# One-token decode layer on one core: K and V in 4 MiB tiles of four heads, 32 KiB a partition, with score tiles by token quarter

## The chip, the core and the metric

The kernel runs on one core of one Trainium2 chip. The metric is the device time of one execution in microseconds. The work is done by TensorE (PE, matrix products, with its weight loads shown apart as PEld), VectorE (DVE), ScalarE (ACT) and GpSimd (POOL); SyncE (SP) only issues transfers. Transfers from device memory (HBM) into the on-chip memory (SBUF, 128 partitions) are carried by 16 DMA engines; matrix products land in PSUM, eight banks of 512 fp32 columns a partition.

## The reference

One token for each of B = 4 sequences goes through a layernorm, attention over a cached window, a second layernorm and a gated feed-forward part:

```python
x = A_x                                              # [4, 1, 576]
q = (layernorm(x) @ wq).reshape(B, 1, 32, 128)       # 32 query heads of 128
k = k_cache[:, :, 16384 - 4096:, :]                  # 16 K/V heads, last 4096 tokens,
v = v_cache[:, :, 16384 - 4096:, :]                  #   two query heads share a K/V head
p = softmax(q @ k.T * 128 ** -0.5)
h = x + (p @ v).reshape(B, 1, 4096) @ wo
g = layernorm(h)
out = h + (relu(g @ W_gate) * (g @ W_up)) @ W_down   # 576 -> 4608 -> 576
```

Everything is bfloat16 in memory. K and V of the window are 64 pairs (sequence, head) of 1 MiB each, so 134.2 MB of the 159.6 MB that the kernel reads; the rest are the weights.

## The kernel before

All engines run programs written out by hand. A small scheduler (`Sched`) counts the instructions of each engine and lets an instruction wait for a named earlier one (`deps`). Every large transfer is issued by SP in one fixed order, the list `transfers`, and SP waits at each transfer until the earlier user of its SBUF place is done (`add`, which finds the places that overlap); what stands behind a waiting transfer waits too.

A "duo" is two K/V heads of one sequence: 2 MiB of K or of V, as 128 partitions of 16 KiB. Partition 2p+s holds 64 consecutive tokens (64p to 64p+63) of head s, one contiguous run of HBM; the two heads of a duo lie 4 MiB apart there. There are 32 duos, four places for K duos and four for V duos. The order is wq (4.7 MB), K0 to K4, then V and K in turn with V five duos behind (`VLEAD`), then wo, the gate and up weights, and the down weights in nine pieces. wo takes the places of the first K duos, the gate and up weights those behind them, and the down weights wait for the product with wo (`ATTN`).

For each half of a K duo (`tr`, line 414) DVE transposes 128 x 2048 fp32 words (each word a pair of bf16) in blocks of 32 x 32 into one of `NKT` = 3 buffers `kT`. PE then does eight products of 128 x 512 (`qk`): the weights are `qz`, q put into the columns of its own duo with zeros elsewhere. Four duos (a batch of 8 K/V heads) accumulate into one score tile `sc` of four banks, 128 rows by 2048 columns. After the batch DVE takes the row maximum (`rmax`, line 417), POOL the maximum over partitions (line 293), DVE the bias (`fbias`), ACT four exponentials of 512 with row sums (line 342), DVE transposes the whole tile of 128 x 2048 fp32 (`trp`, line 433) and ACT casts and packs it to bf16 (line 349). The two heads of a duo lie in alternate columns. The scores of the next batch overwrite `sc` and so wait for the exponentials. The product with V (`pv`) runs five duos behind (`PVLAG`): 16 products of 16 x 512 a duo. PE's order is the scores of duo i, then the product with V of duo i-5. For each batch ACT copies the result (`cpy`), PE adds up the four token parts (`ext`), DVE divides by the sum of the exponentials (`norm`, one for each sequence).

Behind the attention: product with wo, second layernorm, gate and up products, down product in the order in which the nine pieces land, output.

All matrix products are issued by one helper, so they share line 518; they are told apart by tile (`sc<-kT,qz` for the scores, `pb<-pool,prob` for the product with V).

Of the kernel before, what the change touches and what calls it, by code (L numbers as in the profile page):

```python
# [7 lines left out]
ALU = mybir.AluOpType  # L8
# [4 lines left out]
B = 4  # L13
# [6 lines left out]
T = WIN // 64  # L20
# [3 lines left out]
NDUO = B * KVH // 2  # L24
NB = 4
NBATCH = NDUO // NB
NHB = 4 * NB
# [3 lines left out]
DUO = 2 * WIN * DH // 128  # L31
NKS = 4
NVS = 4
# [4 lines left out]
VLEAD = 5  # L38
PVLAG = 5
JJ = 9  # L40
BIG = 1.5e38
NG = FC // JJ
# [60 lines left out]
def bass_sequential_preLN__sliding_block_cached__glu_gated_reglu__decode_kernel(  # L103
# [12 lines left out]
    with ExitStack() as es:  # L116
# [4 lines left out]

        pool = sb("pool", [128, (NKS + NVS) * DUO], BF16)
        kT = sb("kT", [128, NKT, DUO // 4], FP32)
# [6 lines left out]
        x_f = sb("x_f", [B, D], FP32)  # L130
        junk_f = sb("junk_f", [B, D], FP32)
# [12 lines left out]
        qz = sb("qz", [128, 2, NB, 4, 128], BF16)  # L144
        mask = sb("mask", [128, 3, NHB], FP32)
        selT = sb("selT", [128, 4, NHB], FP32)
        rmx = sb("rmx", [128, 2, 2], FP32)
        rsel = sb("rsel", [128, 2], FP32)
        bmin = sb("bmin", [128, 2], FP32)
        pmax = sb("pmax", [128, 2, NHB], FP32)  # L150
        bcm = sb("bcm", [128, 2, NHB], FP32)
        t8 = sb("t8", [128, NHB], FP32)
        bias = sb("bias", [128, 2, 2], FP32)
        rs2 = sb("rs2", [128, 2, 4], FP32)
        rs1 = sb("rs1", [128, 2], FP32)
        P = sb("P", [128, T * 32], FP32)
        probT = sb("probT", [128, T, 32], FP32)
        prob = sb("prob", [128, 2, NB, T, 4], BF16)
# [12 lines left out]
        hhT = probT[:, 0:FC // 2, :].bitcast(BF16).rearrange("p f b -> p (f b)")[:, 0:FC * 32].rearrange("p (f b) -> p f b", b=32)  # L171
        S8 = probT[:, FC // 2:FC // 2 + 16, :].bitcast(BF16).rearrange("p f b -> p (f b)")
# [39 lines left out]
        def duo(cache, d):  # L212
# [3 lines left out]
        def add_K(d):  # L216
            s = d % NKS
            add(("K", d), f"kslot{s}", s * DUO, DUO, ("TR", 2 * d + 1),
                lambda e, o: e.dma_start(out=o, in_=duo(A_k_cache, d)))

        def add_V(d):
            s = d % NVS
            add(("V", d), f"vslot{s}", (NKS + s) * DUO, DUO, ("PV", d),
                lambda e, o: e.dma_start(out=o, in_=duo(A_v_cache, d)))
# [3 lines left out]
        add(("wq", 0), "wq0", NKS * DUO, 4 * HQ, "QMM",  # L228
            lambda e, o: e.dma_start(out=o, in_=A_wq[0:512, :].rearrange("(p u) n -> p (u n)", u=4)))
        add(("wq", 4), "wq4", NKS * DUO + 4 * HQ, HQ // 2, "QMM",  # L230
            lambda e, o: e.dma_start(out=o, in_=A_wq[512:576, :].rearrange("r (u n) -> (r u) n", u=2)))
        for m in range(NDUO + VLEAD):
            if m < NDUO:
                add_K(m)
            if m >= VLEAD:
                add_V(m - VLEAD)
# [36 lines left out]
        def prog_pool(S):  # L273
# [15 lines left out]
            for n in range(NBATCH):  # L289
                deps = [("EMAX", n)]  # L290
                if n >= 2:
                    deps.append(("BIAS", n - 2))
                S.op(g, lambda e, n=n: e.partition_all_reduce(bcm[:, n % 2, :], pmax[:, n % 2, :], 128, bass_isa.ReduceOp.max),  # L293
                     deps=deps, name=("PAR", n))


        def prog_act(S):
# [12 lines left out]
            def qzero(n):  # L310
                b, q = divmod(n, 2)
                for g in range(4):
                    deps = []
                    if g == 0:
                        deps = ["D_QR", "QZ0"] if n < 2 else [("QK", 2 * NB * (n - 1) - 1)]
                    src = bass.AP(tensor=qrep, offset=32 * g * 4 * H * B + NHB * q * B + b,
                                  ap=[[4 * H * B, 32], [4 * B, NB], [H * B, 4], [B, 4]])
                    dst = bass.AP(tensor=qz, offset=32 * g * 2 * NB * 512 + (n % 2) * NB * 512 + 32 * g,
                                  ap=[[2 * NB * 512, 32], [512 + 4, NB], [128, 4], [1, 4]])
                    S.op(a, lambda e, src=src, dst=dst: e.copy(out=dst, in_=src), deps=deps,  # L320
                         name=("QZ", n) if g == 3 else None, signal=g == 3)

            def cpy(n):
                deps = [("PV", NB * n + NB - 1)]
                if n >= 2:
                    deps.append(("EXT", n - 2))
                S.op(a, lambda e: e.copy(out=cp[:, n % 2, :], in_=pb[PVB + n % 2]), deps=deps, name=("CP", n))  # L327
# [3 lines left out]
            for n in range(NBATCH):  # L331

                for th in range(2):
                    for u in range(2):
                        deps = []
                        if th == 0 and u == 0:
                            deps = [("BIAS", n)]
                            if n >= 1:
                                deps.append(("TRP", n - 1))
                            if n >= 2:  # L340
                                deps.append(("RSUM", n - 2))
                        S.op(a, lambda e, n=n, th=th, u=u: e.activation(  # L342
                            out=P[:, th * 1024 + u:(th + 1) * 1024:2], in_=sc[:, th * 1024 + u:(th + 1) * 1024:2], func=ACT.Exp,
                            scale=SCALE, bias=bias[:, n % 2, u:u + 1], accum_out=rs2[:, n % 2, 2 * th + u:2 * th + u + 1]),
                            deps=deps, name=("EXP", n, th) if u else None, signal=u == 1)
                deps = [("TRP", n)]
                if n >= 2:
                    deps.append(("PV", NB * (n - 2) + NB - 1))
                S.op(a, lambda e, n=n: e.copy(out=prob[:, n % 2, :, :, :],  # L349
                                              in_=probT[:, :, 0:NHB].rearrange("p t (r x) -> p r t x", x=4)), deps=deps, name=("CMP", n))  # L350
                if n >= 1:
                    cpy(n - 1)
                if n + 2 < NBATCH:
                    qzero(n + 2)
            cpy(NBATCH - 1)
# [8 lines left out]
        def prog_dve(S):  # L364
# [17 lines left out]
            for x in range(2):  # L382
                S.op(v, lambda e, x=x: e.memset(pb[PVB + x], 0.0), name=f"PVZ{x}")

            S.op(v, lambda e: e.tensor_reduce(out=mask[:, 0, :], in_=bass.AP(tensor=ident_b, offset=0, ap=[[128, 128], [1, NHB], [32, 4]]),
# [6 lines left out]
            for u in range(2):  # L392
                S.op(v, lambda e, u=u: e.tensor_reduce(out=rsel[:, u:u + 1], in_=mask[:, 1, :].rearrange("p (r s h) -> p s r h", s=2, h=2)[:, u, :, :],
                                                       axis=AX.XY, op=ALU.max), deps=["M1"] if u == 0 else [], name=f"RSEL{u}")
# [12 lines left out]
            def tr(i):  # L407
                deps = [land(("K", i // 2))]
                if i >= NKT:
                    deps.append(("QK", i - NKT))  # L410
                x0 = at[("K", i // 2)] + (i % 2) * (DUO // 2)
                src = pool[:, x0:x0 + DUO // 2].bitcast(FP32).rearrange("p (t c k) -> p c t k", c=2, k=32)
                dst = kT[:, i % NKT, :].rearrange("p (c t k) -> p c t k", c=2, k=32)
                S.op(v, lambda e: e.transpose(out=dst, in_=src), deps=deps, name=("TR", i))  # L414

            def rmax(n):
                S.op(v, lambda e: e.tensor_reduce(out=rmx[:, n % 2, :], in_=sc[:, :].rearrange("p (x u) -> p u x", u=2), axis=AX.X, op=ALU.max),  # L417
                     deps=[("QK", 2 * NB * (n + 1) - 1)], name=("RMAX", n))
                rb = bass.AP(tensor=rmx, offset=(n % 2) * 2, ap=[[4, 128], [0, NB], [1, 2], [0, 2]])
                S.op(v, lambda e: e.tensor_tensor(out=pmax[:, n % 2, :].rearrange("p (r s h) -> p r s h", s=2, h=2),  # L420
                                                  in0=mask[:, 1, :].rearrange("p (r s h) -> p r s h", s=2, h=2), in1=rb, op=ALU.min),
                     deps=[("RMAX", n), "M2"] + ([("PAR", n - 2)] if n >= 2 else []), name=("EMAX", n))

            def fbias(n):
                S.op(v, lambda e: e.scalar_tensor_tensor(out=t8[:, :], in0=bcm[:, n % 2, :], scalar=-SCALE, in1=mask[:, 2, :],
                                                         op0=ALU.mult, op1=ALU.max), deps=[("PAR", n)], name=("T8", n))
                S.op(v, lambda e: e.tensor_reduce(out=bmin[:, n % 2:n % 2 + 1], in_=t8[:, :], axis=AX.X, op=ALU.min),
                     deps=[("T8", n)], name=("BMIN", n))
# [276 lines left out]
```

## Time and profile before

| | us |
|---|---|
| three runs of the kernel before | 382.54, 382.57, 382.62; median 382.57 |
| the profiled execution | 382.39 |
| its span, first to last instruction | 381.1 |
| outside of the span | 1.3 |

The page gives for each engine the time in which it was busy; the span in 40 slices (9.5 us each), with the share in which the 16 DMA engines were busy; the queues of the transfers; the chain of work that ended last, followed back from the end; and groups of instructions with their mean time and with what ended the idle time ahead of them. A query of the trace for the transfers in a stretch gives the packets that started there, their bytes, and the time that they took as a share of 16 engines; a query by stretches gives each engine's busy time and the TensorE clock granted (1.00 is full). Every instruction that moves data has its time in the trace; the ends of matrix products are modelled.

### The profile page before, as it was taken

The page shows a single profiled execution, that of the slowest core. Times are in us where ns is not written, and L with a number is a line of the kernel's source. Part 1 is how long each engine was busy: PE and PEld are TensorE (multiplying, and loading weights), DVE is VectorE, ACT ScalarE, POOL GpSimd, SP SyncE. Part 2 cuts the span into 40 slices and gives each one's busy share as a digit, 9 for nine tenths or more (in the row PEclk, how much of TensorE's full clock was granted, in tenths as well). Part 3 has the DMA queues.
Part 4 walks back from the last instruction along what each step waited for, and adds up shares of the span by engine and source line. Part 5 has one row for each costly group of instructions (what it writes and reads, how often), then busy time and mean ns, then how long its engine had stood idle before and what let it go on. Part 6 is the DMA issues. An engine that isn't in the chain of part 4 may idle for free.

```text
span 381.1 us, 3911 instructions
## 1 busy us (share of the span) xinstructions
PE 284.2 (75%) x1701; PEld 124.4 (33%) x1716; DVE 206.3 (54%) x193; ACT 53.5 (14%) x129; POOL 8.2 (2%) x22
## 2 busy tenths in 40 slices
PE   0059749976996699669957995799779996945474
PEld 0053213322432243224322432243224333435341
DVE  0259789369447754774487548644775443042021
ACT  4012050021102110211031103100310021010020
POOL 4100000000000000000000000000000000000000
PEclk9999969998999899989998999899859997975669
DMA  8999999999999999999999999999999999999995
GB/s 331 409 430 428 426 435 420 434 423 428 431 423 433 423 430 425 428 430 426 430 426 428 430 426 425 432 425 430 426 428 432 421 433 420 420 444 432 414 411 227
DMA packets 11985, 159.84 MB, mean 419 GB/s; under 512 B 1336, under 2 KB 1472, under 8 KB 2624
## 3 DMA queue, kind: packets, MB, share of 16 engines
q1 hardware_dynamic: 11960, 159.59, 98.8%
q8 instruction: 13, 0.21, 0.2%
q14 instruction: 4, 0.03, 0.0%
q10 hardware_dynamic: 8, 0.00, 0.0%
HBM read 159.58 MB, written 0.00 MB: 419 GB/s over the span
## 4 chain that ended last, share of the span: by engine, by line
DMA 34%; PE 33%; DVE 20%; issue 5%; ACT 5%; SPq 1%; POOL 1%; POOLq 0%
DMA pool<-in_A_k_cache_dram 27%; PE pb L518 17%; PE sc L518 16%; DVE kT L414 11%; DMA pool<-in_B_W_down_dram 7%; ACT P L342 4%; DVE probT L433 3%; DVE rmx L417 3%; SPq L254 1%; POOL bcm L293 1%; DVE P L475 1%; DVE P L471 0%; DVE bias L429 0%; DVE sel L374 0%; ACT cp L327 0%
## 5 line engine op out<-in xcount | busy, mean ns | idle before, releaser
L414 DVE STREAM_TRANSPOSE kT<-pool 128x2048 f32<-128x2048 f32 x64 | 144.2, 2290 | 55.8 <-DMA pool<-in_A_k_cache_dram 52.9
L518 PE MATMUL sc<-kT,qz 128*128 128x512 bf16 x497 | 132.1, 418 | 50.2 <-DVE kT L414 46.7
L518 PE MATMUL pb<-pool,prob 128*16 128x512 bf16 x512 | 116.5, 388 | 0.0
L518 PEld LDWEIGHTS sc<-kT,qz 128*128 128x128 bf16 x512 | 48.6, 101 | 130.7 <-DVE kT L414 57.6
L518 PEld LDWEIGHTS pb<-pool,prob 128*16 128x16 bf16 x512 | 43.7, 91 | 70.1 <-issue 16.4
L342 ACT ACTIVATE P<-sc,bias 128x512 f32<-128x512 f32 x32 | 22.2, 720 | 174.9 <-DVE bias L429 174.9
L417 DVE TENSOR_REDUCE rmx<-sc 128x2 f32<-128x2048 f32 x8 | 18.3, 2291 | 32.2 <-PE sc L518 32.2
L433 DVE STREAM_TRANSPOSE probT<-P 128x2048 f32<-128x2048 f32 x8 | 18.5, 2312 | 7.9 <-ACT P L342 7.9
L525 PE MATMUL pb<-ident_b,xn_bf 4*128 4x4 bf16 (+1 forms) x5 | 0.4, 180 | 20.8 <-ACT xn_bf L306 20.8
L327 ACT COPY cp<-pb 128x512 f32<-128x512 f32 x8 | 4.7, 585 | 68.3 <-PE pb L518 68.3
L518 PE MATMUL pb<-selT,cp 128*128 128x16 f32 x64 | 8.6, 267 | 4.3 <-ACT cp L327 4.3
L442 DVE RECIPROCAL rs_sb<-pb 128x32 f32<-128x32 f32 x4 | 1.4, 338 | 18.0 <-PE pb L518 18.0
L349 ACT CAST prob<-probT 128x1024 bf16<-128x1024 f32 x8 | 8.4, 1045 | 19.0 <-DVE rs L436 19.0
L518 PEld LDWEIGHTS pb<-selT,cp 128*128 128x128 f32 x64 | 8.9, 205 | 6.3 <-ACT cp L327 5.3
L505 DVE TENSOR_TENSOR P<-pb,P 128x288 bf16<-128x288 f32 (+1 forms) x2 | 0.8, 402 | 17.5 <-PE pb L518 17.5
L518 PE MATMUL sc<-oX,pool 128*128 128x4 bf16 (+1 forms) x160 | 6.6, 177 | 3.7 <-DVE oX L478 3.7
L293 POOL PARTITION_ALL_REDUCE bcm<-pmax x8 | 3.1, 388 | 290.0 <-DVE pmax L420 290.0
L518 PE MATMUL pb<-pool,hnT 128*32 128x288 bf16 (+1 forms) x48 | 4.4, 408 | 6.4 <-DMA pool<-in_B_W_up_dram 6.4
L320 ACT COPY qz<-qrep 32x64 bf16<-32x64 bf16 x32 | 7.8, 244 | 7.3 <-DVE qrep L451 7.0
L518 PE MATMUL pb<-pool,probT 128*4 128x288 bf16 x72 | 5.7, 285 | 4.0 <-DMA pool<-in_B_W_down_dram 3.4
L518 PE MATMUL sc<-pool,hnT 128*32 128x288 bf16 (+2 forms) x112 | 7.3, 375 | 1.4 <-DMA pool<-in_B_W_gate_dram 1.4
L518 PEld LDWEIGHTS sc<-oX,pool 128*128 128x128 bf16 (+1 forms) x160 | 6.5, 123 | 3.9 <-issue 3.8
(107 smaller groups left out, 79.9 us busy)
## 6 DMA issues: line engine op xcount, KB each, us to landing
pool<-in_A_k_cache_dram SPq DMA_DIRECT2D x32, 2048.0 KB, 28.7
pool<-in_A_v_cache_dram SPq DMA_DIRECT2D x32, 2048.0 KB, 26.3
pool<-in_A_wo_dram SPq DMA_DIRECT2D x4, 1152.0 KB, 21.4
pool<-in_B_W_gate_dram SPq DMA_DIRECT2D x1, 4608.0 KB, 23.9
pool<-in_B_W_up_dram SPq DMA_DIRECT2D x1, 4608.0 KB, 29.4
pool<-in_A_wq_dram SPq DMA_DIRECT2D x1, 4096.0 KB, 13.2
pool<-in_B_W_down_dram SPq DMA_DIRECT2D x2, 1296.0 KB, 22.9
pool<-in_B_W_down_dram SPq DMA_DIRECT2D x5, 432.0 KB, 25.5
```

What stands on the lines that cost most here:

```text
L254: lambda e, g0=g0, g1=g1, j0=j0, nj=nj: e.dma_start(out=wd_sb[:, g0:g1, j0 * D:(j0 + nj) * D], in_=B_W_down[g0 * 128 * JJ:g1 * 128 * JJ, : ...
L293: S.op(g, lambda e, n=n: e.partition_all_reduce(bcm[:, n % 2, :], pmax[:, n % 2, :], 128, bass_isa.ReduceOp.max), deps=deps, name=("PAR", n))
L320: S.op(a, lambda e, src=src, dst=dst: e.copy(out=dst, in_=src), deps=deps, name=("QZ", n) if g == 3 else None, signal=g == 3)
L327: S.op(a, lambda e: e.copy(out=cp[:, n % 2, :], in_=pb[PVB + n % 2]), deps=deps, name=("CP", n))
L342: S.op(a, lambda e, n=n, th=th, u=u: e.activation(out=P[:, th * 1024 + u:(th + 1) * 1024:2], in_=sc[:, th * 1024 + u:(th + 1) * 1024:2], f ...
L349: S.op(a, lambda e, n=n: e.copy(out=prob[:, n % 2, :, :, :], in_=probT[:, :, 0:NHB].rearrange("p t (r x) -> p r t x", x=4)), deps=deps, na ...
L414: S.op(v, lambda e: e.transpose(out=dst, in_=src), deps=deps, name=("TR", i))
L417: S.op(v, lambda e: e.tensor_reduce(out=rmx[:, n % 2, :], in_=sc[:, :].rearrange("p (x u) -> p u x", u=2), axis=AX.X, op=ALU.max), deps=[( ...
L433: S.op(v, lambda e: e.transpose(out=probT[:, :, :].rearrange("p t j -> p (t j)"), in_=P[:, :]), deps=[("EXP", n, 1)] + ([("CMP", n - 1)] i ...
L442: S.op(v, lambda e: e.reciprocal(out=rs_sb[:, b, :], in_=pb[OB][:, 64 + b * H:64 + (b + 1) * H]), deps=[("SUM", b)], name=("RS", b))
L475: S.op(v, lambda e: e.tensor_reduce(out=oS.rearrange("p (x b) -> p x b", b=B), in_=oM.rearrange("p (x s b) -> p x b s", s=8, b=B), axis=AX ...
L518: S.op(t, lambda e: e.matmul(o, lhsT=l, rhs=r, start=start, stop=stop, skip_group_check=skip), deps=deps, name=name, signal=name is not None)
```

## The change

- **Tiles.** A "quad" is four K/V heads of one sequence: 4 MiB, 128 partitions of 32 KiB. Partition 4p+s holds 128 consecutive tokens of head s. There are 16 quads and four places of 4 MiB, shared by K and V in the order of the list; the place of a K quad is given back by its fourth transpose, that of a V quad by its product. V is one quad behind K. At the end of the list V13 lies in place 0, K15 in 1, V14 in 2 and V15 in 3; wo goes over places 0 and 1, the gate weights over 1 and 2, the up weights over 2 and 3.
- **Scores.** Each of the four quarters of a K quad is transposed as before (128 x 2048 words, into three buffers) and gives eight products of 128 x 512, all into the same two banks: quarter j of the tokens is written to the rows 32a + 8j + (query head). A quad so has one score tile of 128 x 1024, and two tiles take turns in the four banks. Columns of the four heads lie interleaved.
- **Mask.** Ahead of each tile's products two products of `foe` (4 x 128) and `col` (4 x 512) write a large negative number where the row's head is not the column's head, so the exponential gives zero there. Before, foreign columns were left out by separate exponentials and biases.
- **Softmax by tile.** Maximum over 1024 columns, maximum over partitions, bias, one exponential of 1024 to bf16 with the row sum, one transpose of 128 x 1024 in bf16 into one of four buffers. The cast and packing on ACT, the second bias and the sum of four row sums are gone.
- **Product with V.** 32 products a quad, weights of 128 x 32, the moving operand four runs of 128 columns (one from each quarter of the partition); the result of a sequence (4 quads) fills one bank. Copy, `ext` and `SUM` come once for each sequence.
- `x_f` and `junk_f` now lie in `P`, which is free at that time. The places and the order of wo, gate, up and down weights keep their offsets in SBUF.

```diff
-        pool = sb("pool", [128, (NKS + NVS) * DUO], BF16)
+        pool = sb("pool", [128, NSLOT * QUAD], BF16)
...
-            b, m = divmod(d, KVH // 2)
-            return cache[b, 2 * m:2 * m + 2, SK - WIN:SK, :].rearrange("s (p t) d -> p s (t d)", p=64)
+            b, m = divmod(i, NPB)
+            return cache[b, NS * m:NS * m + NS, SK - WIN:SK, :].rearrange("s (p t) d -> p s (t d)", p=32)
...
+        slots = iter(range(2 * NQUAD))
+
+        def add_K(i):
+            x = next(slots) % NSLOT
+            add(("K", i), f"slot{x}", x * QUAD, QUAD, ("TR", 4 * i + 3),
+                lambda e, o: e.dma_start(out=o, in_=quad(A_k_cache, i)))
+
+        def add_V(i):
+            x = next(slots) % NSLOT
+            add(("V", i), f"slot{x}", x * QUAD, QUAD, ("PV", i),
...
+        for m in range(NQUAD + VLEAD):
+            if m < NQUAD:
                 add_K(m)
             if m >= VLEAD:
                 add_V(m - VLEAD)
...
+            for i in range(NQUAD):
+                deps = [("BIAS", i)]
+                if i >= 2:
+                    deps += [("TRP", i - 2), ("RSUM", i - 2)]
+                S.op(a, lambda e, i=i: e.activation(
+                    out=Pb[:, (i % 2) * 1024:(i % 2 + 1) * 1024], in_=sc[:, (i % 2) * 1024:(i % 2 + 1) * 1024], func=ACT.Exp,
+                    scale=SCALE, bias=bias[:, i % 2:i % 2 + 1], accum_out=rs1[:, i % 2:i % 2 + 1]),
+                    deps=deps, name=("EXP", i))
+                if i + 2 < NQUAD:
+                    qzero(i + 2)
+                if i >= NPB and i % NPB == 0:
+                    cpy(i // NPB - 1)
...
+            def trp(i):
+                b, m = divmod(i, NPB)
+                S.op(v, lambda e: e.transpose(out=pT[i % NPT], in_=Pb[:, (i % 2) * 1024:(i % 2 + 1) * 1024]),
+                     deps=[("EXP", i)] + ([("PV", i - NPT)] if i >= NPT else []), name=("TRP", i))
...
+            for i in range(NQUAD):
+                for j in range(4):
+                    tr(i, j)
...
+                rmax(i)
+                fbias(i)
+                trp(i)
+                if i > NPB and i % NPB == VLEAD:
+                    norm(i // NPB - 1)
...
+            def qk(i, j):
+                f = 4 * i + j
+                bank = 2 * (i % 2)
+                deps = [("TR", f)]
+                if j == 0:
+                    for half in range(2):
+                        mm(pb[bank + half], foe[:, :], col[:, :], True, False, deps=(["COL"] if i == 0 else [("EXP", i - 2)] if i >= 2 else []) if half == 0 else [])
+                    deps.append(("QZ", i))
+                for ce in range(4):
+                    c, e = divmod(ce, 2)
+                    for half in range(2):
...
+            def pv(i):
+                b, r = divmod(i, NPB)
+                x0 = at[("V", i)]
+                vv = pool[:, x0:x0 + QUAD].rearrange("p (q t d) -> p t q d", q=4, d=DH)
+                deps = [("TRP", i), land(("V", i))]
+                if r == 0 and b >= 2:
+                    deps.append(("CP", b - 2))
+                for t_ in range(TQ // 4):
...
+            for i in range(NQUAD + VLEAD):
+                if i < NQUAD:
+                    for j in range(4):
+                        qk(i, j)
+                if i >= VLEAD:
+                    j = i - VLEAD
+                    if j % NPB == 0 and j >= NPB:
+                        ext(j // NPB - 1)
+                    pv(j)
```

More of the change, by code (lines that the diff above doesn't have):

```diff
@@ L329, in prog_act, with cpy @@
+            def cpy(b):
+                deps = [("PV", NPB * b + NPB - 1)]
+                if b >= 2:
+                    deps.append(("EXT", b - 2))
+                S.op(a, lambda e: e.copy(out=cp[:, b % 2, :], in_=pb[PVB + b % 2]), deps=deps, name=("CP", b))
             qzero(0)
             qzero(1)
[L331 to L354, printed above, removed]
@@ L416, in rmax @@
[L416 to L422, printed above, removed]
```

262 lines of the change are left out of this document (102 added, 160 removed).

## The prediction

> **What bounds the kernel now.** I read the page's transfers first, then what SP and the engines do around the last V duo.
>
> ```profile
> PE 284.2 (75%) x1701; PEld 124.4 (33%) x1716; DVE 206.3 (54%) x193; ACT 53.5 (14%) x129; POOL 8.2 (2%) x22
> ...
> DMA  8999999999999999999999999999999999999995
> ...
> q1 hardware_dynamic: 11960, 159.59, 98.8%
> ...
> pool<-in_A_k_cache_dram SPq DMA_DIRECT2D x32, 2048.0 KB, 28.7
> pool<-in_A_v_cache_dram SPq DMA_DIRECT2D x32, 2048.0 KB, 26.3
> ```
>
> SP's queue (q1) keeps all 16 DMA engines busy for 98.8% of the span; the missing 1.2% (4.6 us) lie in the first and the last slice. A K or V duo lands 26 to 29 us after its issue, though its own share of the traffic is about 5 us: over 20 us of other transfers always stand ahead of it. PE is busy 75%, DVE 54%. So the time is that of the bytes through the DMA engines, plus start and end, and the waits between engines cost nothing while the queue has a stock. A change can win only by making the transfers cheaper, and lose by letting the queue run dry or making the transfers dearer.
>
> The tail, from the order of instructions in time:
>
> ```profile
> 328.62 0.33 SPq L243 DMA_DIRECT2D pool<-in_B_W_gate_dram  x1
> 334.03 0.59 ACT L327 COPY cp<-pb 128x512 f32<-128x512 f32 x1 [16.06 <-PE pb L518]
> 334.09 0.33 SPq L243 DMA_DIRECT2D pool<-in_B_W_up_dram  x1
> ...
> 340.97 6.63 PE L518 MATMUL sc<-oX,pool 128*128 128x4 bf16 x160 [3.67 <-DVE oX L478]
> 347.63 17.50 SPq L254 DMA_DIRECT2D pool<-in_B_W_down_dram  x9
> ...
> 352.56 0.91 PE L518 MATMUL sc<-pool,hnT 128*32 128x216 bf16 x16 [1.42 <-DMA pool<-in_B_W_gate_dram]
> ...
> 363.52 0.37 PE L518 MATMUL pb<-pool,hnT 128*32 128x216 bf16 x4 [6.42 <-DMA pool<-in_B_W_up_dram]
> ```
>
> The up weights are issued when the last product with V ends (334.1) and land at 363.5; the down weights are issued at 347.6, 16 us ahead of that landing. The end of attention is thus covered by queued weights, and gate, up and down products wait for data.
>
> **The price of a row.** The same query of the transfers for three stretches: one with 16 KiB rows of K and V, one in which 32 KiB rows of wq start, one with mostly 36 KiB rows of gate and up.
>
> ```profile
> DMA packets 7345, 106.97 MB, mean 428 GB/s; under 512 B 815, under 2 KB 815, under 8 KB 815
> ...
> q1 hardware_dynamic: 7336, 106.84, 100.5%
> ```
> ```profile
> DMA packets 65, 2.13 MB, mean 426 GB/s; under 512 B 0, under 2 KB 0, under 8 KB 0
> ...
> q1 hardware_dynamic: 65, 2.13, 98.7%
> ```
> ```profile
> DMA packets 239, 7.78 MB, mean 432 GB/s; under 512 B 19, under 2 KB 19, under 8 KB 27
> ...
> q1 hardware_dynamic: 236, 7.74, 100.3%
> ```
>
> The first is 60 to 310 us: 7336 packets, 815 of them the small end marks of a transfer (16 each), so 6521 rows. They took 1.005 x 16 x 250 = 4020 us of engine time: 616.5 ns a row with its share of the marks. The second is 4 to 9 us: 65 rows took 0.987 x 16 x 5 = 79.0 us, 1215 ns each. The third is 342 to 360 us: 209 rows of 36 KiB (236 less 19 marks and 8 rows of 4.5 KiB) took 1.003 x 16 x 18 = 288.9 us, less some 1.6 us for the small ones, 1374 ns each. A row therefore carries a small fixed cost: 32 KiB cost 2 x 616.5 = 1233 ns in two rows and 1215 in one. If the 36 KiB row is scaled by bytes alone, with no fixed part, 32 KiB cost 1222 ns; that stretch has the engines at work as the K and V stretch has, while at 4 to 9 us PE and DVE stand still.
>
> **The change part by part.**
>
> *Transfers.* 64 issues of 128 rows become 32. Each DMA engine carries 64 x 128 / 16 = 512 rows of K and V now, 256 of double size after. The gain a 32 KiB row is 1233 - 1222 = 11 ns at least and 1233 - 1215 = 18 ns at most; I take 14, between them, since the quiet row is too cheap for a busy stretch and the scaled one leaves out that the fixed part is paid once. The marks are halved too, which is inside the 1233. 256 x 14 ns = 3.6 us (2.8 to 4.6). Half the issues on SP (0.54 to 0.61 us each) are hidden by the stock and gain nothing.
>
> *Does the queue stay full?* A quad's K and V take 16 rows an engine, 16 x 1.219 = 19.5 us. The softmax chain of the second batch, from the chain of work, and the groups:
>
> ```profile
> 74.00 3.74 PE sc L518 x16
> ...
> 77.77 2.30 DVE rmx L417
> ...
> 80.37 0.40 POOL bcm L293
> ...
> 81.46 2.86 ACT P L342 x8
> ...
> 84.35 2.31 DVE probT L433
> ...
> 86.97 2.23 DVE kT L414
> 89.19 0.05 issue
> 89.24 3.37 PE sc L518 x8
> ```
> ```profile
> L414 DVE STREAM_TRANSPOSE kT<-pool 128x2048 f32<-128x2048 f32 x64 | 144.2, 2290 | 55.8 <-DMA pool<-in_A_k_cache_dram 52.9 <-PE sc L518 2.9
> ...
> L508 DVE STREAM_TRANSPOSE probT<-P 128x288 bf16<-128x288 bf16 x4 | 1.9, 478 | 0.1
> ...
> L471 DVE TENSOR_TENSOR P<-sc,mask 128x1024 f32<-128x1024 f32 x1 | 1.2, 1225 | 0.7 <-PE sc L518 0.7
> ```
>
> From the maximum to the next K transpose before takes 86.97 - 77.77 = 9.2 us. After, a tile has half the columns: maximum 1.2 (DVE reads 1024 fp32 of PSUM in 1.225 us), exponential 1.4 (half of 2.86; at most the 2.86), transpose of 1024 bf16 1.25 (the 288 one's 0.48 plus 736 columns at the slope to the 2.31 of 2048; between 1.15 and 2.31), the rest as now less one small step, 1.5: 5.4 us, at most 7.9. DVE's loop over a quad is four transposes of 2.29 (9.2), the products of the fourth quarter (eight, half of 3.74, 1.9) and these 5.4: 16.5 us, 19.0 by the upper ends, under 19.5 both times. PE has 32 score products, 32 with V and 2 masks of about 3.74 / 16 = 0.23 us: 15.4 us. The masks (0.5 us a quad) stand ahead of PE's wait for the first transpose and need only the exponential of two quads earlier, so they lie in PE's idle time; uncovered they would be 16 x 0.47 = 7.5 us. They cannot gain. The moving operand of `pv` in runs of 128 columns and its 32-column weights have no row; the scores read every second element now and go at the same 0.23, so I take no cost. It becomes visible only if 64 such products a quad push PE past 19.5 us, that is at 0.30 us each. The cast, `BMIN`, second bias and `RS1` removed lie beside the stream: nothing.
>
> *The places.* The start, in time order, and the first stretch:
>
> ```profile
> 22.38 2.30 DVE L414 STREAM_TRANSPOSE kT<-pool 128x2048 f32<-128x2048 f32 x1
> ...
> 27.03 0.69 DVE L451 CAST qrep<-sc 128x512 bf16<-128x512 f32 x1 [0.70 <-PE sc L518]
> ...
> 27.76 2.05 ACT L320 COPY qz<-qrep 32x64 bf16<-32x64 bf16 x8 [7.03 <-DVE qrep L451]
> ```
> ```profile
> 0.00:14.00 14.00, 0.00 (x0) 0.00 (x0) 0.58 (x4) 4.30 (x7) 3.88 (x7) 1.00 0.88 349
> ```
>
> Four places of 4 MiB hold the same bytes as eight of 2 MiB. The tightest is the first reuse by K3 (place of K1). wq and five quads stand ahead of it, 25.7 MB: 4.9 in the first 14 us (349 GB/s), the rest at 428 until about 62 us. K0 (wq and 4.2 MB) lands near 24 us rather than 22; q is ready at 27.7 and put into `qz` by some 30, so the fourth quarter's scores end near 38, the chain adds 5.4 and K1's four transposes 9: 53 us, 9 us ahead. With loops of 16.5 against 19.5 this grows. V1 and V2 have 12 us or more.
>
> *The tail.* In the last places wo waits for V13 and K15, gate for V14, up for V15. The last product is one of a quad now, 32 x 0.23 = 7.4 us behind V15's landing, about 4 us later against its data than the duo's 16; up has wo and gate (9.4 MB, 22 us) ahead of it in the queue. The down weights wait for `ATTN`, 13.6 us behind the last product before (334.0 to 347.6), and had 16 us of cover. Cost nothing; without that cover up to 4 us.
>
> Sum: 382.39 - 3.6 = 378.8 for the profiled execution, which lies 0.2 under the median of the runs; so 379.0 for the median, 378.0 to 379.8 by the ends of the row's price.
>
> **The rivals.**
>
> *The stream gets no cheaper.* The 18 ns are then what compute adds to a row in proportion to its bytes (PE and DVE use SBUF beside it), not a price per row; the marks alone are left. The 36 KiB row, measured beside work, speaks against it. Time 382.3: within 0.2%.
>
> *A cold TensorE makes the quad longer than its transfers* (slower). The stretches show the clock falling to half after 3.5 us of idle PE:
>
> ```profile
> 85.75:89.50 3.75, 0.26 (x2) 0.14 (x3) 3.71 (x5) 1.04 (x1) 0.00 (x0) 1.00 1.05 441
> 89.50:92.91 3.41, 3.41 (x9) 0.93 (x8) 3.41 (x2) 0.00 (x0) 0.00 (x0) 0.50 0.96 408
> ```
>
> After the change PE ends its product with V and waits for the next K quad and its first transpose in every quad, some 4 us (19.5 less 15.4), so this can come each 19.5 us rather than each 39. One stretch of 3.41 us at half clock costs 1.7 us of PE work: 17.1 us for PE, 18.2 for the loop, still covered. It decides from two such stretches on in every quad with the upper ends of the chain: 19.0 + 3.4 = 22.4 us, 2.9 over, 16 times 46 us, less the 9 us ahead at the start: 379 + 37 = 416; with the middle of the chain, 16.5 + 3.4 = 19.9, the stock covers it. Half way, 21.2 us a quad, 16 x 1.7 - 9 = 18 us: 397, the time I give it. The stock of two quads and the short idle speak against.
> The Trainium skill, "TensorE: Matmul & The Clock Gate", Part 1, says that an idle window of about 3.4 us throttles the clock to half until a busy one has passed; the trace agrees with 3.75 us ahead of 3.41 at 0.50.
>
> *Four heads make the reads slower* (slower). Rows of neighbouring partitions lie 4 MiB apart in HBM, in pairs now, in fours after, and an engine may have several in flight. That pairs cost nothing visible (616.5 against half of 1215) speaks against, and wq has no such step. A slow 32 KiB row is seen at the start: from 1.5 to 13.5 us the stream made 384 GB/s, against 428 later.
>
> ```profile
> DMA packets 252, 4.61 MB, mean 384 GB/s; under 512 B 19, under 2 KB 23, under 8 KB 124
> ```
>
> If K and V went at that, 134.2 MB would take 349 us, not 314: 382.6 + 35 = 418. It loses as soon as a row costs over 1233 ns.
> The Trainium skill, "DMA: Bandwidth & Descriptors", Latency and other measured facts, gives 103 GB/s for copies with rows 4 MiB apart where 214 is full; by that, an estimate, K and V would take twice as long. The pairs at 428 GB/s here disagree, and no run yet shows four.
>
> **How the numbers follow.** A measurement of this kernel can tell 0.2%, 0.8 us, from no change. The forecast, 379.0, has 0.78; the stream unchanged 0.08; the cold TensorE 0.08; slow reads 0.06. So faster 0.78, same 0.08, slower 0.14. The forecast's own range is 378.0 to 379.8; for 8 in 10 I go down to 377.5 (the shares are read to 0.1%, near 1 ns a row, and the engines end unevenly) and up to 382.6, which takes in the unchanged stream and leaves out the slower cases.
>
> **What would show it.** Right: 32 KiB rows of K and V at 1215 to 1222 ns; q1 again near 98.8% of a shorter span; DVE waiting for K in every quad; up weights issued over 20 us ahead of their landing. Wrong: a slice of DMA under 9 between the first and the last (a dry queue; the time from issue to landing then falls to some 10 us); rows over 1233 ns; half clock in a large part of the slices together with DVE no longer waiting for K.

## The result, and the profile after

| | before | after |
|---|---|---|
| median of the runs, us | 382.56 (382.26 to 382.62, 4 runs) | 380.29 (380.21 to 380.30, 4 runs) |
| ratio, with its 95% interval | | 0.9942 (0.9925 to 0.9959) |
| profiled execution, us | 382.39 | 380.29 |
| its span, us | 381.1 | 379.0 |
| mean TensorE clock | 0.909 | 0.909 |

The kernel became faster by 2.27 us. 3.6 us were forecast.

The page of the kernel after: busy times, the line of the DMA engines over the span, the queue, the chain by engine, the groups that the prediction priced, and the issues of K and of the up weights.

```profile
PE 296.7 (78%) x1716; PEld 129.4 (34%) x1716; DVE 210.2 (55%) x223; ACT 49.5 (13%) x117; POOL 11.0 (3%) x30
...
DMA  8999999999999999999999999999999999999995
...
q1 hardware_dynamic: 7352, 159.59, 98.5%
...
DMA 59%; DVE 22%; PE 14%; ACT 1%; SPq 1%; issue 1%; POOL 0%
...
L404 DVE STREAM_TRANSPOSE kT<-pool 128x2048 f32<-128x2048 f32 x64 | 142.5, 2281 | 38.9 <-DMA pool<-in_A_k_cache_dram 38.6
...
L337 ACT ACTIVATE P<-sc,bias 128x1024 bf16<-128x1024 f32 x16 | 17.8, 1114 | 248.5 <-DVE bias L415 248.5
L407 DVE TENSOR_REDUCE rmx<-sc 128x1 f32<-128x1024 f32 x16 | 19.6, 1225 | 41.2 <-PE sc L497 41.2
L420 DVE STREAM_TRANSPOSE probT<-P 128x1024 bf16<-128x1024 bf16 x16 | 19.9, 1245 | 20.3 <-ACT P L337 20.3
...
L497 PE MATMUL sc<-col,foe 4*128 4x512 bf16 x32 | 10.0, 394 | 0.0
...
pool<-in_A_k_cache_dram SPq DMA_DIRECT2D x16, 4096.0 KB, 29.9
...
pool<-in_B_W_up_dram SPq DMA_DIRECT2D x1, 4608.0 KB, 25.8
```

The queue is still the bound: q1 is busy for 98.5% of a span that is 2.1 us shorter, no slice between the first and the last falls under 9, and the chain that ended last is mostly DMA. The packets of q1 fell from 11960 to 7352 for the same 159.59 MB. DVE waits 38.6 us for K, so compute is not late. PE grew by 12.5 us of busy time (10.0 us are the 32 mask products; the page before has a record of only 497 of the 512 score products), and none of this shows in the time.

The transfers from 60 to 310 us of the kernel after, in the same query that gave 428 GB/s before:

```profile
DMA packets 3708, 107.69 MB, mean 431 GB/s; under 512 B 416, under 2 KB 416, under 8 KB 416
...
q1 hardware_dynamic: 3698, 107.55, 100.1%
```

3698 packets less 416 marks are 3282 rows of 32 KiB. 250 us on 16 engines are 4000 us, so a row, with its share of the marks, occupies an engine for 1218.8 ns.

### The profile page after: what moved, and what is told of

Read it like the earlier page. It is cut to its first block, busy times and chain, and to the rows that moved or that the text cites. A ratio compares the mean times of both kernels' runs of the same rounds, so it can differ in the third digit from the quotient of the medians.

```text
span 379.0 us, 3903 instructions
## 1 busy us (share of the span) xinstructions
PE 296.7 (78%) x1716; PEld 129.4 (34%) x1716; DVE 210.2 (55%) x223; ACT 49.5 (13%) x117; POOL 11.0 (3%) x30
## 3 DMA queue, kind: packets, MB, share of 16 engines
q1 hardware_dynamic: 7352, 159.59, 98.5%
## 4 chain that ended last, share of the span: by engine, by line
DMA 59%; DVE 22%; PE 14%; ACT 1%; SPq 1%; issue 1%; POOL 0%
DMA pool<-in_A_k_cache_dram 53%; DVE kT L404 18%; PE sc L497 10%; DMA pool<-in_B_W_down_dram 6%; PE pb L497 4%; DVE probT L420 1%; DVE rmx L407 1%; ACT P L337 1%; SPq L256 1%; DVE P L454 1%; DVE P L450 0%; ACT qz L322 0%; POOL bcm L295 0%; DVE pmax L409 0%; DVE qrep L436 0%
## 5 line engine op out<-in xcount | busy, mean ns | idle before, releaser
L497 PE MATMUL sc<-kT,qz 128*128 128x512 bf16 x512 | 141.8, 437 | 41.1 <-DVE kT L404 40.0
L404 DVE STREAM_TRANSPOSE kT<-pool 128x2048 f32<-128x2048 f32 x64 | 142.5, 2281 | 38.9 <-DMA pool<-in_A_k_cache_dram 38.6
L497 PE MATMUL pb<-pool,probT 128*32 128x512 bf16 (+1 forms) x584 | 118.9, 368 | 5.3 <-DMA pool<-in_B_W_down_dram 3.9
L497 PEld LDWEIGHTS sc<-kT,qz 128*128 128x128 bf16 x512 | 51.8, 106 | 131.0 <-DVE kT L404 55.6
L497 PEld LDWEIGHTS pb<-pool,probT 128*32 128x32 bf16 (+1 forms) x584 | 50.9, 95 | 71.5 <-DMA pool<-in_B_W_down_dram 7.6
L337 ACT ACTIVATE P<-sc,bias 128x1024 bf16<-128x1024 f32 x16 | 17.8, 1114 | 248.5 <-DVE bias L415 248.5
L407 DVE TENSOR_REDUCE rmx<-sc 128x1 f32<-128x1024 f32 x16 | 19.6, 1225 | 41.2 <-PE sc L497 41.2
L420 DVE STREAM_TRANSPOSE probT<-P 128x1024 bf16<-128x1024 bf16 x16 | 19.9, 1245 | 20.3 <-ACT P L337 20.3
L322 ACT COPY qz<-qrep 32x128 bf16<-32x128 bf16 x64 | 18.8, 294 | 10.4 <-DVE qrep L436 9.8
L504 PE MATMUL pb<-ident_b,xn_bf 4*128 4x4 bf16 (+1 forms) x5 | 0.4, 180 | 19.5 <-ACT xn_bf L308 19.5
L497 PE MATMUL sc<-col,foe 4*128 4x512 bf16 x32 | 10.0, 394 | 0.0
L504 PEld LDWEIGHTS pb<-ident_b,xn_bf 4*128 4x128 bf16 (+1 forms) x5 | 0.3, 115 | 19.5 <-ACT xn_bf L308 19.5
L497 PEld LDWEIGHTS pb<-selT,cp 128*128 128x128 f32 x32 | 4.1, 191 | 1.7 <-ACT cp L329 1.2
## 6 DMA issues: line engine op xcount, KB each, us to landing
pool<-in_A_k_cache_dram SPq DMA_DIRECT2D x16, 4096.0 KB, 29.9
pool<-in_B_W_up_dram SPq DMA_DIRECT2D x1, 4608.0 KB, 25.8
pool<-in_B_W_down_dram SPq DMA_DIRECT2D x2, 1296.0 KB, 19.4
```

Of the source, the lines that this page charges most:

```text
L337: S.op(a, lambda e, i=i: e.activation(out=Pb[:, (i % 2) * 1024:(i % 2 + 1) * 1024], in_=sc[:, (i % 2) * 1024:(i % 2 + 1) * 1024], func=ACT ...
L407: S.op(v, lambda e: e.tensor_reduce(out=rmx[:, i % 2:i % 2 + 1], in_=sc[:, (i % 2) * 1024:(i % 2 + 1) * 1024], axis=AX.X, op=ALU.max), dep ...
L420: S.op(v, lambda e: e.transpose(out=pT[i % NPT], in_=Pb[:, (i % 2) * 1024:(i % 2 + 1) * 1024]), deps=[("EXP", i)] + ([("PV", i - NPT)] if ...
L497: S.op(t, lambda e: e.matmul(o, lhsT=l, rhs=r, start=start, stop=stop, skip_group_check=skip), deps=deps, name=name, signal=name is not None)
```

## The experiments

The theory at this point: a row (one contiguous run into one partition) has a fixed price beside its bytes, the kernel after has 256 rows less on each engine, and nothing else in the change moves the time. Rival A: what is saved goes with the number of transfers (32 instead of 64, with their marks). Rival B: the lighter softmax on DVE and ACT lets the stream run faster. Rival C: compute is close to the stream, so that the margin is about to be lost. All runs stand beside runs of the kernel before on the same chip (medians 382.58, 382.66 and 382.64 on three chips).

**The kernel after once more.** No edit.

> The changed kernel as it is, beside the three variants. Theory (a row of a K or V transfer has a fixed cost of some 7 ns on its DMA engine, whatever its length, and halving the rows is the whole gain): 380.3 us, 0.6% under the kernel before. Every rival expects the same.

Measured: 380.27 us (380.07 to 380.39), ratio 0.9933 (0.9918 to 0.9947). The gain is there on another chip; this is the number beside which the next ones stand.

**Rows of 16 KiB in the kernel after.** Two transfers for each tile, each with one half of the bytes of all 128 partitions. All the compute is that of the kernel after.

```diff
-                lambda e, o: e.dma_start(out=o, in_=quad(A_k_cache, i)))
+                lambda e, o: pieces(e, o, quad(A_k_cache, i)))     # V likewise
+        def pieces(e, o, src):
+            w = QUAD // 2
+            return tuple(e.dma_start(out=o[:, x * w:(x + 1) * w], in_=src[:, :, x * w:(x + 1) * w]) for x in range(2))
```

> Each 4 MiB tile is brought by two transfers of 128 partitions with rows of 16 KiB: rows and transfers as before (8192 and 64), compute as after. Theory of the row: 256 more rows an engine at 7 ns and 32 marks at 9 ns, 2.1 us: 382.4 us, equal to the kernel before. Rival of the number of transfers: 382.4 us too, but then the run with two transfers of 32 KiB rows shows it as well. Rival of the lighter compute (fewer and smaller steps on DVE and ACT disturb the transfers less): 380.3 to 380.6 us.

Measured: 382.56 us, ratio 0.9997 (0.9988 to 1.0006). The whole gain is gone although quads, masks and the softmax by tile are all still there. Rival B falls: compute has no part in it that this interval would show. Rows and number of transfers both went back here, so A stands yet.

**Rows of 16 KiB, 32 transfers.** One transfer of 4 MiB whose partitions each get two rows of 16 KiB, of two neighbouring heads. The scores and sums thereby mix tokens of different heads, so the output is not that of the layer; bytes, transfers and instructions are those of the kernel after.

```diff
-            ...rearrange("s (p t) d -> p s (t d)", p=32)
+            ...rearrange("s (p t) d -> p s (t d)", p=64)
```

> One transfer of 4 MiB a tile as after, but with two rows of 16 KiB in each partition (64 tokens of one head and 64 of the next; the scores are then summed over tokens dealt to other heads, at the same cost). 8192 rows, 32 transfers, compute as after. Theory of the row, with the price from the runs so far (2.29 us for 256 rows and 32 marks an engine, marks at 9 ns, so 7.8 ns a row): 2.0 us more than after, 382.3 us. Rival, the gain is in the number of transfers: 380.3 us.

Measured: 382.56 us, ratio 0.9997 (0.9989 to 1.0006). Transfers from 60 to 310 us:

```profile
DMA packets 6943, 106.93 MB, mean 428 GB/s; under 512 B 415, under 2 KB 415, under 8 KB 415
...
q1 hardware_dynamic: 6933, 106.79, 100.4%
```

Half as many marks as before (415, not 815), the same rate as before (428 GB/s), the same time as before. It is the rows.

**Rows of 32 KiB, 64 transfers.** The counterpart: two transfers for each tile, one to the even partitions and one to the odd ones.

```diff
+        def halves(e, o, src):
+            return (e.dma_start(out=o[0:128:2, :], in_=src[:, 0:4:2]), e.dma_start(out=o[1:128:2, :], in_=src[:, 1:4:2]))
```

> Rows of 32 KiB, two transfers a tile, each to every second of the 128 partitions instead of to one half of them. Theory of the row: 32 more marks an engine, 0.3 us: 380.6 us. Rival of the number of transfers: 382.5 us. If what made the transfers to partitions 0 to 63 and 64 to 127 slow (212 GB/s) lies in there being 64 partitions and not in their being one half, some 700 us.

Measured: 380.13 us, ratio 0.9932 (0.9918 to 0.9946); the stretch from 60 to 310 us:

```profile
DMA packets 4111, 107.65 MB, mean 431 GB/s; under 512 B 820, under 2 KB 820, under 8 KB 820
...
q1 hardware_dynamic: 4101, 107.52, 100.0%
```

Twice the transfers and twice the marks cost nothing that shows. With the run before this one, rival A falls from both sides: 32 transfers of short rows give the old time, 64 transfers of long rows the new one.

**Rows of 8 KiB, in both kernels.** In the kernel after four transfers for each quad (`QUAD // 4` in `pieces`), in the kernel before two for each duo (`DUO // 2`); 128 transfers in both.

> Four transfers a tile with rows of 8 KiB: 768 more rows an engine than after, 96 more marks. Theory of the row: 768 x 7 ns + 96 x 9 ns = 6.2 us: 386.5 us. Rival of the number of transfers (2 us for each 32 of them): 386.3 us, told apart by the two runs above. Rival of the lighter compute: 381.2 us, the marks alone.

> The kernel before with rows of 8 KiB: two transfers a duo, each 128 x 8 KiB; 16384 rows and 128 transfers, compute as before. Theory of the row: as from 16 to 8 KiB under the compute of after (4.79 us): 387.4 us. Rival, the compute of before has a price of its own beside the rows: clearly different from 387.35 us, the same rows under the compute of after.

Measured: 387.35 us for the new compute (ratio 1.0117, 1.0098 to 1.0135) and 387.34 us for the old (1.0123, 1.0108 to 1.0138). With equal rows the medians of the two kernels, on two chips, lie 0.01 us apart, while the runs of either spread over 0.3 to 0.6 us; this speaks against rival B a second time. The stretch from 60 to 310 us of the new compute with 8 KiB rows:

```profile
DMA packets 14447, 105.27 MB, mean 421 GB/s; under 512 B 1604, under 2 KB 1604, under 8 KB 1604
...
q1 hardware_dynamic: 14436, 105.13, 101.1%
```

14436 less 1604 are 12832 rows in 4000 us: 311.7 ns each, 1246.9 for 32 KiB in four rows. The price of a further row by all of these:

| step | rows more an engine | us | ns a row |
|---|---|---|---|
| 32 to 16 KiB, 380.27 to 382.56 (one chip) | 256 | 2.29 | 8.9 |
| 16 to 8 KiB, 382.56 to 387.35 (the same chip) | 512 | 4.79 | 9.4 |
| 32 to 16 KiB, 380.13 to 382.56 (second chip) | 256 | 2.43 | 9.5 |
| before to after, 382.56 to 380.29 | 256 | 2.27 | 8.9 |

It is one price, 9 ns or a little more, over a factor of four in the size of a row. By the count of rows the second row of 32 KiB costs 8.0 ns (1226.8 less 1218.8), and the third and fourth 10.0 each; but one row more or fewer on each engine at the ends of the stretch would move the price of 32 KiB by 3 to 6 ns, so the times are the better measure. The steps also differ in end marks (32 more an engine in the first, 64 more in the second, 32 fewer in the third), and this leaves no trace in the price. What in a row takes the 9 ns no run here shows.

**Halves of the partitions.** This was meant as the first test of the number of transfers: rows of 32 KiB, one transfer to partitions 0 to 63 and one to 64 to 127. The second form takes other heads, so another order of the reads in HBM (its output is not the layer's).

```diff
+        def halves(e, o, src):
+            return (e.dma_start(out=o[0:64, :], in_=src[0:16]), e.dma_start(out=o[64:128, :], in_=src[16:32]))
# second form:
+            return (e.dma_start(out=o[0:64, :], in_=src[:, 0:2]), e.dma_start(out=o[64:128, :], in_=src[:, 2:4]))
```

> Each 4 MiB tile is brought by two transfers of 64 partitions with rows of 32 KiB: rows as after, transfers as many as before (64), compute as after. Theory of the row: only 32 more end marks an engine, 0.3 us: 380.6 us. Rival, the gain is in the number of transfers and their end marks: 382.4 us, all of it lost. Rival, the gain is in the lighter compute: 380.3 us.

> Rows of 32 KiB, two transfers a tile to partitions 0 to 63 and 64 to 127, but each engine reads the rows of two heads over all tokens instead of four heads over half of them (the tile's rows lie in other partitions, so the sums are over tokens of other heads). If the half of the partitions is what made the earlier run slow: 700 us again, 212 GB/s. If it was the order of the reads in HBM: 380.5 us.

Measured: 700.42 us for the first (ratio 1.829, 1.824 to 1.834), 704.26 for the second, in a single run. Transfers of the first from 60 to 310 us:

```profile
DMA packets 2024, 53.04 MB, mean 212 GB/s; under 512 B 402, under 2 KB 402, under 8 KB 402
...
q1 hardware_dynamic: 2018, 52.95, 100.3%
```

All 16 engines are busy, at half the rate: 2018 less 402 are 1616 rows, 2475 ns each. The kernel with every second partition has the same number of transfers, of rows and of partitions in each, and runs at 431 GB/s; so neither the number of transfers nor that a transfer has 64 partitions is the cause, but which 64. The order in HBM is not it either, since both forms are slow.
The Trainium skill, "SBUF — State Buffer", Door 1: The DMA port swizzle, says that the bandwidth of a transfer goes by how many of the 16 ports into SBUF its partitions reach, and that partitions 0 to 63 reach eight. The trace agrees: 212 GB/s beside 431, and 431 again where even partitions are spread over all 128.

**Without the masks.** The two mask products of each tile are left out (foreign heads then enter the softmax, and the output is not the layer's); the wait for the exponential stays at the first score product.

```diff
-                        mm(pb[bank + half], foe[:, :], col[:, :], True, False, ...)
-                        mm(pb[bank + half], qz[...], kv_[...], False, j == 3 and ce == 3, ...)
+                        mm(pb[bank + half], qz[...], kv_[...], j == 0 and ce == 0, j == 3 and ce == 3, ...)
```

> The 32 mask products are left out, so that foreign heads count in the softmax (the output is not that of the reference). Theory, transfers set the end and the masks lie in the idle time of TensorE: 380.3 us. Rival, the masks cost on the path: up to 10 us less (their busy time in the profile after), 370.3 us.

Measured: 380.22 us, ratio 0.9933 (0.9920 to 0.9946). The 10.0 us of mask products are hidden in full.

**Two, four and six more maxima for each tile.** DVE repeats the row maximum of 1024 columns into a scratch column, ahead of the real one. This makes the loop of a quad longer by a known step and changes nothing else in the program.

```diff
+                for _ in range(2):           # 4, 6
+                    S.op(v, lambda e, _=_: e.tensor_reduce(out=extra[:, _:_ + 1], in_=sc[...], axis=AX.X, op=ALU.max),
+                         deps=[("QK", 4 * i + 3)], signal=False)
```

> Two more row maxima of 1024 columns a tile on VectorE, in the chain between scores and exponential: 2.5 us a quad. Theory, the loop of a quad takes some 16.7 us (maximum at 39.49, next K transpose at 44.45, four transposes 8.9, last products 2.9) and its transfers 19.5: 19.2 us is still under, 380.3 us. Rival, the loop is already the bound: 16 x 2.5 = 40 us more, 420 us; if it lies just under it, some 385 us.

> Four more row maxima a tile. With two, the loop of a quad on VectorE took 18.6 us (193.55 to 212.12 in that run) of which 2.36 us were the two; four make it 20.9 us against transfers of 19.5. Theory, the transfers bound the time until the loop is longer than they and the stock of some 10 us is used up: 15 x 1.4 - 10 = 11 us more, 391 us. Rival, transfers and loop hardly overlap at the margin (any chain over the transfers shows in full): 380.3 + 22 = 402 us. If the stock is larger than I count, 380.3 us.

> Six more row maxima a tile: 23.3 us a quad, 3.8 us over. Theory: 15 x 3.8 - 10 = 47 us more, 427 us, and 36 us more than with four; DMA idle in many slices, and VectorE never waiting for K data that had landed early. Rival, PE is what sets the loop: less than half of that difference.

Measured: 380.15 us with two (ratio 0.9932, 0.9920 to 0.9945), 408.75 with four (1.0690, 1.0672 to 1.0708), 453.33 with six (1.1852, 1.1832 to 1.1872). DVE's transposes of K in time order tell where they differ. First the kernel after: the fourth and the fifth quad, two quads in the middle and the last:

```profile
76.87 8.88 DVE L404 STREAM_TRANSPOSE kT<-pool 128x2048 f32<-128x2048 f32 x4
...
94.32 8.89 DVE L404 STREAM_TRANSPOSE kT<-pool 128x2048 f32<-128x2048 f32 x4 [1.50 <-DMA pool<-in_A_k_cache_dram]
...
210.89 8.89 DVE L404 STREAM_TRANSPOSE kT<-pool 128x2048 f32<-128x2048 f32 x4 [2.51 <-DMA pool<-in_A_k_cache_dram]
...
230.30 8.89 DVE L404 STREAM_TRANSPOSE kT<-pool 128x2048 f32<-128x2048 f32 x4 [3.02 <-DMA pool<-in_A_k_cache_dram]
...
308.95 8.89 DVE L404 STREAM_TRANSPOSE kT<-pool 128x2048 f32<-128x2048 f32 x4 [2.97 <-DMA pool<-in_A_k_cache_dram]
```

With two more maxima, the last one:

```profile
308.58 8.89 DVE L405 STREAM_TRANSPOSE kT<-pool 128x2048 f32<-128x2048 f32 x4 [1.02 <-DMA pool<-in_A_k_cache_dram]
```

With four, the first and the last:

```profile
24.83 2.31 DVE L405 STREAM_TRANSPOSE kT<-pool 128x2048 f32<-128x2048 f32 x1 [3.11 <-DMA pool<-in_A_k_cache_dram]
...
344.85 8.88 DVE L405 STREAM_TRANSPOSE kT<-pool 128x2048 f32<-128x2048 f32 x4
```

From the fifth quad on the kernel after goes by its data: a wait for K in front of each quad, 19.4 us a quad. With two more maxima (2.4 us) only the first and the last three quads wait for K; the last still waits 1.0 us and starts at 308.58 us, no later than the 308.95 of the kernel after. With four no wait for K is left behind the first; 15 loops lie between 24.83 and 344.85, 21.33 us each, against 19.5 for a quad's transfers (16 x 1.219). The excess is 1.83 us a quad, 16 x 1.83 = 29.3 us, and 28.5 were measured over 380.27. Six maxima add 44.6 us to that, 2.8 for each of 16 quads. The added maxima take 6.88 us a quad with six and 4.62 with four, 2.26 more. Nearly all of the rest is DVE's wait for the last score products of a quad, 7.4 us longer in all or 0.46 a quad. With four, then with six:

```profile
DVE extra L409 <- PE sc L501: 44.8, 16, 3.7
```
```profile
DVE extra L409 <- PE sc L501: 52.2, 16, 3.8
```

The mean granted clock of TensorE fell as well, from 0.883 to 0.853; that it makes these products late is likely, but no run sets it apart.

The expectation for four had counted an excess of 15 x 1.4 = 21 us, had taken a stock of 10 us off it, and so came to 391 us. The page of that kernel (DMA slices and their rates, queue, issues of K and of the up weights) shows what happened; the issues on SP are those of the gate and the up weights:

```profile
DMA  9999999999999999999999999999999999839996
GB/s 358 402 439 434 428 437 418 444 418 420 425 392 402 429 354 421 417 396 389 373 375 428 409 400 372 412 389 386 372 396 405 392 400 372 356 136 443 405 395 250
...
q1 hardware_dynamic: 7352, 159.59, 95.3%
...
pool<-in_A_k_cache_dram SPq DMA_DIRECT2D x16, 4096.0 KB, 15.0
...
pool<-in_B_W_up_dram SPq DMA_DIRECT2D x1, 4608.0 KB, 16.6
```
```profile
363.73 0.33 SPq L246 DMA_DIRECT2D pool<-in_B_W_gate_dram  x1
373.28 0.33 SPq L246 DMA_DIRECT2D pool<-in_B_W_up_dram  x1
```

The shares of the engines stay at 9 nearly to the end of attention (the first slice under 9 is the 35th, from 346 us on), but they hide the loss: from the ninth slice to the 36th no rate reaches 431 GB/s (from 60 to 310 us it is 403 at a share of 98.0%), and a K quad lands 15.0 us after its issue (median) rather than 29.9. The stock shrinks while the loop runs. The places of the last V quads come free when their products end, at 373.3 rather than 335.6 us, so the up weights are issued 37.7 us late. 9.2 us of this come back, because the up weights then land 16.6 us after their issue and not 25.8; 28.5 remain. So a stock near the 10 us that the expectation counted was used up. Its mistake was the lag, 37.7 us and not 21: the loop took 21.33 us rather than 20.9, and it has to be set against 18.9 us and not 19.5, since the first quads of the kernel after run ahead of their transfers (15 loops from 25.35 to 308.95 us). That lead (15 x 0.6 = 9 us) and the 9.2 us of the stock nearly cancel, and so the time grew by about 16 times the 1.83 us. Rival C is thus bounded: the margin is over 2.4 us a quad and under 4.9, and from four to six maxima each us a quad cost 16.

## Why the prediction was right or wrong

**What bounds the kernel: right.** The time goes by the queue before and after, and by equal rows the two computations take equal times (387.35 and 387.34; 382.56 for 16 KiB rows with either).

**The price of a row: right in kind, too large.** This is the step that failed. The saving was put at 14 ns a 32 KiB row, between 11 and 18; it is 9, outside of these ends, so that 380.29 lies above the forecast's own range of 378.0 to 379.8, though inside of 377.5 to 382.6, which was wide enough to take in the unchanged stream as well. The term "1.005 x 16 x 250 = 4020 us of engine time" is at fault. 16 engines have 4000 us in 250; a share over 100% says that recorded packets overlap, or in a short stretch that they run over its end, not that an engine gave more time than there is. With 4000, a 16 KiB row is 613.4 ns, two are 1226.8. The 36 KiB row was taken in the same way, at 100.3%: with 288 us, less the 1.6, it is 1370.3 ns, and 1218.1 for 32 KiB by bytes. The difference is 8.7 ns, 256 times 2.2 us, and the forecast would have been 380.2 us for the profiled execution; 380.29 came. That this is so near is partly luck: the 36 KiB row rests on 209 rows in 18 us, some 13 an engine, and one row more or fewer on each engine at its ends would move the price by some 100 ns. The row of 32 KiB itself was foreseen well, between 1215 and 1222, and is 1218.8; it was the old row that was priced 6 ns too high, and the quiet row of 1215 that pulled the choice up. The overlap grows with the number of packets: 100.1% with 3698 of them, 100.4% with 6933, 101.1% with 14436.

**Number of transfers and issues: nothing, as forecast.** 64 transfers of 32 KiB rows: 380.13. The end marks, which the forecast had inside the price of a row, do not show either.

**The chain and the loop: right.** DVE in time order, from the first K transpose to the second quad:

```profile
25.35 2.31 DVE L404 STREAM_TRANSPOSE kT<-pool 128x2048 f32<-128x2048 f32 x1 [4.15 <-DMA pool<-in_A_k_cache_dram]
...
39.49 1.23 DVE L407 TENSOR_REDUCE rmx<-sc 128x1 f32<-128x1024 f32 x1 [3.13 <-PE sc L497]
...
44.45 8.89 DVE L404 STREAM_TRANSPOSE kT<-pool 128x2048 f32<-128x2048 f32 x4
```

From the maximum of the first tile to the next K transpose it took 4.96 us, forecast 5.4. Maximum, exponential and transpose were put at 1.2, 1.4 and 1.25 us and are 1.225, 1.114 and 1.245. Where the loop waits for no data it takes 15.8 to 16.6 us, forecast 16.5: the second to the fourth quad start at 44.45, 61.03 and 76.87 us, and the fifth, with 1.50 us of waiting, at 94.32. For the same reason one of the signs named ahead, a wait of DVE for K in every quad, is missing in these three: their K has landed already. It stands in all the others.

**The masks: hidden, as forecast;** but a product takes 0.31 us of busy PE (10.0 us / 32) rather than the 0.23 that were assumed.

**The places: right.** The issue of K3, in time order on SP, stands at the forecast 53 us:

```profile
53.37 0.54 SPq L221 DMA_DIRECT2D pool<-in_A_k_cache_dram  x1
```

K0's first transpose starts at 25.35 us, forecast 24, and no slice runs dry.

**The tail: right.** SP's issues and PE's wait for the up weights, of the kernel after:

```profile
335.61 0.33 SPq L245 DMA_DIRECT2D pool<-in_B_W_up_dram  x1
...
349.22 13.77 SPq L256 DMA_DIRECT2D pool<-in_B_W_down_dram  x9
```
```profile
361.42 0.37 PE L497 MATMUL pb<-pool,hnT 128*32 128x216 bf16 x4 [3.26 <-DMA pool<-in_B_W_up_dram]
```

The up weights go out 1.5 us later than before, when the last product ends, and still land 2.1 us earlier, 25.8 us after their issue. The down weights are issued 12.2 us ahead of that landing (15.9 before), so the cover held.

**The rivals.** The unchanged stream: no, rows of 16 KiB bring the old time back under the new compute. Slow reads of four heads: no, 431 GB/s. The cold TensorE came, but had no effect. Three stretches around the start of the last quad and one over the quad ahead of it, in the kernel after (length; busy time of PE, PEld, DVE, ACT, POOL; granted clock; DMA share; GB/s):

```profile
307.90:311.31 3.41, 0.61 (x3) 0.11 (x2) 2.36 (x2) 0.00 (x0) 0.00 (x0) 0.84 1.00 432
311.31:314.72 3.41, 3.41 (x9) 1.16 (x10) 3.41 (x2) 0.00 (x0) 0.00 (x0) 0.50 0.96 413
314.72:318.00 3.28, 3.28 (x11) 1.24 (x10) 3.12 (x2) 0.00 (x0) 0.00 (x0) 0.64 0.95 410
289.58:309.00 19.42, 16.56 (x66) 6.47 (x66) 12.09 (x11) 1.20 (x2) 0.36 (x1) 0.91 1.00 431
```

PE waits for the first transpose and then works at half clock, as that rival said. By the shares of the three stretches (0.84, 0.50, 0.64), if the clock is either full or half, it is at half for some 6.9 us there, two of the rival's 3.41 us; over the quad ahead, at 0.91, for some 3.5 us. That quad has PE busy for 16.56 of 19.42 us, so it is covered. The price that the rival was given (397, with 9 us of stock taken off) was too low: by the run with four maxima the time grows by about 16 times the excess, with nothing off in sum. At 21.2 us a quad it would have been 16 x 1.7 = 27 us more, about 407.

## What to carry to other kernels

Where the queue is the bound, a change is worth what it does to the rows: here 9 ns for each row saved on an engine, whatever the number of transfers and whatever the compute, as long as its loop stays under the loop of the data. Take the price of a row from time and count (16 engines x stretch / rows), not from shares of recorded time, which can be over 100%, and over a stretch so long that a row at its ends does not matter. A full share is no sign of a full rate either: 98.0% went with 403 GB/s under four more maxima, and 100.3% with 212 GB/s where the partitions were halved. A stock of loaded tiles did not save a loop that is too long by the same amount every time: here the time grew by about 16 times the excess over a quad's transfers, since the lag is still there when the last tile is done.

## What the runs showed of the hardware that was not expected

- A transfer to one half of the partitions runs at half the rate: 212 GB/s with all 16 engines shown as busy (700.42 us in all), 431 GB/s with every second partition. Splitting a tile in two is free by even and odd partitions and costs 320 us here by halves.
- The fixed price of a row is nearly the same down to 8 KiB: 1218.8 ns for 32 KiB in one row, 1226.8 in two, 1246.9 in four. The end marks and the issue of a transfer cost nothing that can be seen behind a full queue.
- Four heads with rows 4 MiB apart in HBM, on neighbouring partitions, load at full rate (431 GB/s).
